# A Fourier convolution with two mixtures of experts behind it: the first batch in the planned order, weights decoded without GpSimd

## The chip, the core and the metric

The kernel runs on one core of a Trainium2 chip. TensorE (PE) multiplies, VectorE (DVE), ScalarE (ACT) and GpSimd (POOL) work on tiles, and every transfer is issued by the queue of SyncE (SP), in order. The metric is the device time of one execution in microseconds (us).

## The reference, cut to what matters

```python
X = np.fft.rfft(x, axis=1)                      # x: 8 x 3072 x 256
y = np.fft.irfft(X * (filt_r + 1j * filt_i)[None], n=3072, axis=1)
x = y.reshape(8 * 3072, 256)
h = x @ w_in                                     # 256 x 2048, float64 weights
x = (h / (1 + np.exp(-h)) @ w_out).astype(np.float32)
logits = x @ phi                                 # 32 slots, 8 experts
d = softmax(logits, axis=0); c = softmax(logits, axis=1)
slots = d.T @ x                                  # 32 x 256
slots = relu(slots[e] @ w1[e]) @ w2[e]           # for each expert e
return c @ slots
```

## The kernel before

**Fourier part.** A batch of 3072 tokens is 24 x 128. Stage 1 makes 12 products `pa` of tiles x and cosines c (128 x 256 and 128 x 128 each), folds them into `ea` and stores that in DRAM (scratch s1). Stage 2, in four quarters Q, gathers `a` from s1 (four transfers of 24 rows x 8 KB a quarter), multiplies it with `em` into four banks `px` (U = 0 to 3) and scales by the filter `f`: y = px * f_r on VectorE (direct), sw = the two halves of px exchanged and signed on ScalarE, times f_i on GpSimd (cross), and y + sw on VectorE. Stage 3 multiplies y with `gm` into four banks `pb`, copies them to `eb` and stores those in s2. Stage 4, for each chunk of 512 tokens (six a batch, 48 in all), loads `b` from s2, adds signs (`bp`, `b`, called fly in the code), multiplies with `d` into `py` and splits the result into `yT`, high and low part.

**Expert part.** For each chunk 16 blocks m of six products `ph` of yT and w_hl (w_in, split in high and low), silu `g` on ScalarE, a transpose X of g on VectorE, and the logits `pl`, 128 products of g with `wp` = w_out phi, made once. The soft mixture sums exp(logits) with X (`pd`, with the tile `E`, which comes through DRAM as `ed`) into `acc` on VectorE. After the last chunk a tail runs the experts and writes the output.

**Weights.** w_in and w_out arrive as float64, as pairs of 32-bit words. `decode` turns 512 columns (a quarter) into float32: ScalarE takes the high word's magnitude, VectorE does four operations on 128 x 1024, ScalarE converts part of the low word, and GpSimd multiplies and adds (four operations of 128 x 512). `split_w` makes w_hl. For `wp`, `make_wp` multiplies w_out (transposed) with phi, and PE transposes the same tile for the tail: it goes to DRAM as `wos` and comes back as `wo`, one transfer of 2 MB.

**Order.** A list `plan` holds (t, function); t is in slots, 16 to a chunk, and the functions run in the order of t. Each engine then works in that order, and SP issues its transfers in it. Batches 1 to 7 are planned (`fft_plan`), one batch ahead of its chunks, so that their stages stand between hidden products. Batch 0 stands as code (`fft_first`) at t = -20: for each Q it issues four gathers, then three filter loads; its products stand as px0, px1, pb0, px2, pb1, px3, pb2, pb3.

## Time and profile before

| | us |
|---|---|
| median of 3 runs | 1971.06 (1967.1 to 1977.47) |
| the profiled execution | 1971.93 |
| its span | 1970.2 |
| PE busy | 1848.9 (94% of the span) |
| DVE / ACT / POOL busy | 1287.9 / 951.0 / 340.5 |
| moved by the DMA engines | 264.36 MB, 134 GB/s on average |
| mean granted clock of PE | 0.959 of full speed |

The execution lasts 1.7 us longer than its span, which runs from the first to the last record. A share of the whole span is a mean over stages with different limits: the rows further down are therefore by stage. A row of a timeline has the start, the duration, the engine, the line, the operation with its output and input, how many instructions it joins, and in brackets how long the engine had been idle before it and what it had waited for.

### The profile page before, as it was taken

The numbers are of one execution on the slowest core, as the hardware profiler recorded it, in microseconds if no ns is written. First come the engines' busy times: TensorE is split into PE (matmuls) and PEld (weight loads), VectorE is DVE, ScalarE is ACT, GpSimd is POOL, SyncE is SP. The second block draws the span as 40 slices with busy tenths as digits, with TensorE's granted clock in tenths as the row PEclk, the third lists the DMA queues.
The fourth block names the chain that finished last, engine by engine and source line by source line (L and its number), as shares of the span: only waits on it lengthen the run. The fifth ranks groups of instructions, "written<-read, shape, count | busy, mean of one in ns | idle before, by whom it ended". The sixth has DMA issues, their size and how long they took to land. (4 is left out here: it accounts for less than half of the span.)

```text
span 1970.2 us, 49869 instructions
## 1 busy us (share of the span) xinstructions
PE 1848.9 (94%) x21108; PEld 1385.5 (70%) x21108; DVE 1287.9 (65%) x2207; ACT 951.0 (48%) x1816; POOL 340.5 (17%) x248
## 2 busy tenths in 40 slices
PE   4569999999999999999999999999999999999985
PEld 2157677877787777877777777767787777777643
DVE  4777666767767775767676776676676774555443
ACT  3444455555454564554554545545544644343322
POOL 3653211212121220221121121121121210000000
PEclk7679999999999999999999999999999999999886
DMA  9745533445254443453253533453344513311669
GB/s 280 207 176 177 127 88 106 131 135 130 57 157 130 120 116 86 144 139 105 71 176 107 131 95 110 147 150 83 102 140 125 143 54 120 100 35 37 210 234 386
DMA packets 186943, 264.36 MB, mean 134 GB/s; under 512 B 18784, under 2 KB 144096, under 8 KB 179424
## 3 DMA queue, kind: packets, MB, share of 16 engines
q1 hardware_dynamic: 186720, 261.17, 44.6%
q8 instruction: 166, 2.72, 0.6%
q14 instruction: 57, 0.47, 0.1%
HBM read 177.80 MB, written 83.30 MB: 133 GB/s over the span
## 5 line engine op out<-in xcount | busy, mean ns | idle before, releaser
L61 PE MATMUL ph<-yT,w_hl 128*128 128x512 f32 x4608 | 1096.2, 393 | 2.1 <-ACT g L593 1.7
L61 PEld LDWEIGHTS ph<-yT,w_hl 128*128 128x128 f32 x4608 | 851.4, 188 | 204.9 <-issue 25.8
L603 DVE STREAM_TRANSPOSE X<-g 128x512 f32<-128x512 f32 x768 | 515.6, 694 | 206.0 <-ACT g L593 205.6
L593 ACT ACTIVATE g<-ph 128x512 f32<-128x512 f32 x768 | 454.6, 608 | 350.0 <-PE ph L61 305.2
L237 POOL TENSOR_TENSOR sw<-sw,f 128x512 f32<-128x512 f32 x128 | 180.0, 1430 | 739.2 <-DVE X L603 346.1
L571 ACT ACTIVATE yT<-py 128x512 fp32r<-128x512 f32 x96 | 57.4, 598 | 366.9 <-PE py L61 366.9
L61 PE MATMUL pd<-X,E 32*32 32x512 f32 x6144 | 226.1, 611 | 3.5 <-DMA E<-ed 3.1
L61 PEld LDWEIGHTS pl<-g,wp 128*32 128x32 f32 x6144 | 163.4, 110 | 72.8 <-issue 50.6
L61 PE MATMUL pl<-g,wp 128*32 128x128 f32 x6144 | 191.3, 275 | 4.1 <-issue 4.0
L290 POOL TENSOR_TENSOR xh<-x,xh 128x512 fp32r<-128x512 f32 x84 | 111.9, 1333 | 465.8 <-DVE xh L289 445.7
L61 PEld LDWEIGHTS pd<-X,E 32*32 32x32 f32 x6144 | 119.4, 104 | 81.9 <-issue 46.9
L687 DVE SCALAR_TENSOR_TENSOR acc<-acc,nm,pd 128x512 f32<-128x512 f32 x188 | 127.2, 738 | 34.4 <-PE pd L61 33.9
L572 DVE TENSOR_TENSOR yT<-py,yT 128x512 fp32r<-128x512 f32 x96 | 66.4, 691 | 59.4 <-ACT yT L571 59.1
L360 DVE TENSOR_TENSOR y<-y,sw 128x512 f32<-128x512 f32 x112 | 104.8, 975 | 0.0
L61 PE MATMUL pa<-xh,ch 128*128 128x256 f32 x504 | 76.4, 287 | 9.9 <-ACT wp L146 9.7
L234 DVE TENSOR_TENSOR y<-px,f 128x512 f32<-128x512 f32 x120 | 78.9, 677 | 10.2 <-ACT sw L227 8.7
L61 PEld LDWEIGHTS pa<-xh,ch 128*128 128x128 f32 x504 | 72.4, 192 | 18.5 <-ACT wp L146 10.0
L61 PE MATMUL py<-d,b 128*128 128x128 f32 x416 | 68.4, 290 | 17.9 <-DMA b<-s 11.6
L554 DVE SCALAR_TENSOR_TENSOR bp<-b,sg 128x512 f32<-128x512 f32 (+1 forms) x48 | 34.9, 727 | 69.9 <-DMA b<-s 69.3
L226 ACT ACTIVATE sw<-px,sg 128x256 f32<-128x256 f32 x128 | 64.6, 505 | 33.0 <-DVE y L232 14.7
L633 ACT ACT_TABLE_LOAD x48 | 61.6, 1283 | 37.2 <-DVE nm L626 26.2
L61 PE MATMUL pb<-y,gm 32*32 32x512 f32 (+1 forms) x1072 | 70.1, 627 | 9.2 <-DVE y L464 5.6
(126 smaller groups left out, 1286.4 us busy)
## 6 DMA issues: line engine op xcount, KB each, us to landing
f<-in_filt_dram SPq DMA_DIRECT2D x128, 256.0 KB
x<-in_x_dram SPq DMA_DIRECT2D x96, 256.0 KB
a<-s SPq DMA_DIRECT2D x128, 192.0 KB
s<-eb SPq DMA_DIRECT2D x128, 192.0 KB
out_dram<-ots SPq DMA_DIRECT2D x40, 512.0 KB
d<-in_dmat_dram SPq DMA_DIRECT2D x48, 256.0 KB
wt<-in_w_dram SPq DMA_DIRECT2D x12, 1024.0 KB
E<-ed SPq DMA_DIRECT2D x188, 64.0 KB
```

The lines of the kernel that those rows point to most:

```text
L61: T.matmul(o, lhsT=l, rhs=r, start=start, stop=stop)
L226: A.activation(sw[:, 0, :], p[:, 1, :], AF.Copy, scale=sg[:, s:s + 1])
L234: V.tensor_tensor(y, p, f[:, 0, :].unsqueeze(1).to_broadcast([P, 2, CH]), op=ALU.mult)
L237: G.tensor_tensor(sw, sw, f[:, 1, :].unsqueeze(1).to_broadcast([P, 2, CH]), op=ALU.mult)
L290: G.tensor_tensor(h[:, 1, :], tf, h[:, 0, :], op=ALU.subtract)
L360: V.tensor_tensor(y, y, st.pop(("sw", Q, U)), op=ALU.add)
L571: A.activation(y[:, half, 0, :], py, AF.Copy)
L572: V.tensor_tensor(y[:, half, 1, :], py, y[:, half, 0, :], op=ALU.subtract)
L593: A.activation(g, pht.pop((c, m)), AF.Silu)
L603: V.transpose(xt[c][:, m].rearrange("p b j -> p (b j)"), gt[c, m])
L633: A.activation(t[:, 0], L, AF.Exp, bias=nm[:, 1:2], accum_out=nm[:, 2:3])
L687: V.scalar_tensor_tensor(out=acc[:, :, a, :], in0=acc[:, :, a, :], scalar=mrun[c][:, 3:4], in1=p, op0=ALU.mult, op1=ALU.add)
```

## The change

- **Batch 0 is planned.** `first_plan` puts every step of batch 0 in the list, by microseconds turned into slots. The gathers and filter loads alternate one by one; quarter 0 of the words of w_in is loaded before the stores of stage 1, quarter 1 between those stores and the first gather, quarters 2 and 3 behind the filters and between the stores of s2.
- **Stage 3 takes y and sw apart.** For batch 0 each is multiplied with gm, into the same banks: 32 products a quarter instead of 16, and no addition on VectorE. For U = 3 sw is made by two operations on VectorE straight from px, so GpSimd has three crosses a quarter.
- **Decoding without GpSimd.** One operation on VectorE multiplies the low word by its exponent and a second one adds; ScalarE's conversion is gone too (the magnitude on ScalarE and the four operations before it stay, now in `dec_act` and `dec_dve`). Quarter 3 of w_in and all of w_out are decoded after the first hidden products, between the transposes X, which wait for them there.
- **wp with phi standing.** Eight products of 128 columns a quarter, and one 128 x 128 transpose on VectorE. The transposes on PE, their copies on ScalarE and the way through `wos` are gone.
- **Cosines split beforehand.** Batches 1 to 7 load the high and low part (256 KB a unit instead of 128 KB); ScalarE copies both in one operation and VectorE's subtraction is gone. The tag c has two buffers instead of four, so the load of unit u stands behind the split of unit u - 2 instead of u - 3. The 12 units of batch 1 start 5.2 slots later and lie closer.
- **w_out for the tail.** Four loads of 1 MB of w_out in its own layout come in chunks 41 to 46 and are decoded there (8 operations on ScalarE, 48 on VectorE, of 128 x 512). The weights of experts 0 and 1 are loaded later.

```diff
-            ld=3, c=4, ch=2, xh=2, ev=1, a=1, f=2, sw=1, y=2, ev8=1, bl=1, bp=1, dl=1, wt=3)
+            ld=3, c=2, ch=2, xh=2, ev=1, a=1, f=2, sw=1, y=2, ev8=1, bl=1, bp=1, dl=1, wt=3)
...
-            A.activation(f, top, AF.Copy, scale=2.0 ** -36)
-            for h in range(2):
-                G.tensor_tensor(f[:, h], f[:, h], e[:, h].bitcast(F32), op=ALU.mult)
-                G.tensor_tensor(f[:, h], f[:, h], b[:, h].bitcast(F32), op=ALU.add)
...
+    def load_words(key, q):
+        for h in range(2):
+            src = w_in if key == "in" else w_outT
+            DQ.dma_start(words[key, q][:, h].rearrange("p f w -> p (f w)"),
+                         src[h * P:h * P + P, 512 * q:512 * q + 512].bitcast(U32))
...
+    def dec_low(key, q, out=None):
+        b, e = temps.pop((key, q))
+        t = words[key, q]
+        f = t[:, :, :, 0].bitcast(F32)
+        V.scalar_tensor_tensor(out=f, in0=t.bitcast(U16)[:, :, :, 1], scalar=2.0 ** -36, in1=e.bitcast(F32),
+                               op0=ALU.mult, op1=ALU.mult)
+        V.tensor_tensor(f if out is None else out, f, b.bitcast(F32), op=ALU.add)
...
-        for m in range(4):
-            for h in range(2):
-                mm(pw[:, m, :], f[:, h, m * P:(m + 1) * P], phi_f[:, h, :], h == 0, h == 1)
-        A.activation(wp[:, 4 * q:4 * q + 4, :], pw, AF.Copy)
-        for v in range(2):
-            pt = ps_f.tile([P, 2, CH], F32, tag="pf", name=f"pt_{q}{v}")
-            for m in range(2):
-                for h in range(2):
-                    o = (2 * v + m) * P
-                    T.transpose(pt[:, m, h * P:h * P + P], f[:, h, o:o + P], idt)
-            ev = wk.tile([P, 2, CH], F32, tag="E4", bufs=BUFS["E4"], name=f"wo_{q}{v}")
-            A.activation(ev, pt, AF.Copy)
-            DQ.dma_start(wos[:, 4 * q + 2 * v:4 * q + 2 * v + 2, :], ev)
...
+        f = words["out", q][:, :, :, 0].bitcast(F32).rearrange("p h (m k) -> p h m k", k=P)
+        pwt[q] = pw = ps_f.tile([P, 4 * S], F32, tag="pf", name=f"pw_{q}")
+        for h in range(2):
+            for g in range(4):
+                mm(pw[S * g:S * g + S], phi_f[:, h, :], f[:, h, :, S * g:S * g + S], h == 0, h == 1)
+    def put_wp(q):
+        V.transpose(wp[:, 4 * q:4 * q + 4, :].rearrange("p m s -> p (m s)"), pwt.pop(q))
...
+    def stage3(ps, ys, Q):
+        def special(part):
+            n = 2 * len(ys)
+            for i in range(n):
+                mm(ps[0][0:S, part, :], gm[0:S, 1 + 2 * part + i % 2, :], ys[i // 2][0][0:S, i % 2, :], i == 0, i == n - 1)
+        for i, y in enumerate(ys):
+            for U in range(4):
+                for q in range(4):
+                    if (Q, U, q) == (0, 0, 0):
+                        special(0) if i == 0 else None
+                    else:
+                        mm(ps[q][S * U:S * U + S], gm[S * q:S * q + S, 0, :], y[U][S * q:S * q + S],
+                           i == 0, i == len(ys) - 1)
         if Q == 0:
-            for n in range(1, 4):
-                special(n)
+            special(1)
...
-            c = fp.tile([P, 2, P], F32, tag="c", bufs=BUFS["c"], name=f"c_{b}_{u}")
-            DQ.dma_start(c, cmat[:, 2 * u:2 * u + 2, :])
+            c = fp.tile([P, 2, 2, P], F32, tag="c", bufs=BUFS["c"], name=f"c_{b}_{u}")
+            DQ.dma_start(c, chl[:, 2 * u:2 * u + 2])
...
-            A.activation(ch[:, 0], c, AF.Copy)
-            V.tensor_tensor(ch[:, 1], c, ch[:, 0], op=ALU.subtract)
+            A.activation(ch, c, AF.Copy)
...
-            at(max(t - 7, ts[u - 3] + 0.4) if u > 2 else t1[0] - 9 + u, load1, u)
+            at(max(t - 7, ts[u - 2] + 0.4) if u > 1 else t1[0] - 9 + u, load1, u)
...
+        def load2(Q, U):
+            gather2(st["s1"], st["aa"][:, Q], Q, U)
...
+        def act2(Q, U):
+            k = 4 * Q + U
+            tag = (("ld", "ch", "f", "ev"), ("ld", "ch", "f", "sw"))[Q % 2][U]
+            sws[k] = fp.tile([P, 2, CH], F32, tag=tag, bufs=BUFS[tag], name=f"sw_0_{k}")
+            p = ps["px", Q, U]
+            if U < 3:
+                scale_act(p, sws[k], st["f0"] if k == 0 else None)
+            else:
+                for i in range(2):
+                    V.scalar_tensor_tensor(out=sws[k][:, i, :], in0=p[:, 1 - i, :], scalar=sg[:, i:i + 1],
+                                           in1=fs[k][:, 1, :], op0=ALU.mult, op1=ALU.mult)
...
+        def mat3(Q):
+            for q in range(4):
+                ps["pb", Q, q] = ps_h.tile([P, 2, CH], F32, tag="ph", name=f"pb_0_{Q}{q}")
+            pb = [ps["pb", Q, q] for q in range(4)]
+            stage3(pb, [[t[4 * Q + U] for U in range(4)] for t in (ys, sws)], Q)
...
+                t = 22 + 0.4 * Q + 0.1 * U
+                at(us(t + 0.05), loadf, 4 * Q + U)
+                at(us(t), load2, Q, U)
...
+            t = 33 + 6.3 * Q
+            at(us(t), mat2, Q)
+            for U in range(4):
+                at(us(t + 1.2 + 0.7 * U), direct2, Q, U)
+                at(us(t + (1.3, 2.2, 3.1, 4)[U]), act2, Q, U)
+                if U < 3:
+                    at(us(t + 2.3 + 1.3 * U), cross2, Q, U)
+            t += 6.4
+            at(us(t), mat3, Q)
+            for q in range(4):
+                eng = (A, A, A, V) if Q < 3 else (A, V, A, V)
+                at(us(t + (2.3, 2.8, 3.3, 3.35)[q]), out3, Q, q, eng[q])
+            at(us(t + 4), store3, Q)
...
+        at(us(25.9), loadd, 0)
+        for q, (t0, t1, t2, t3, t4, t5) in enumerate(((5, 22, 23.2, 26.5, 29, 30.2), (21, 28.5, 31, 38.3, 44.8, 44.9),
+                                                      (43, 61, 61.9, 63, 65, 66), (49, 73, 75, 76.5, 79, 80.2))):
+            at(us(t0), load_words, "in", q)
+            at(us(t1), dec_act, "in", q, "a" if q % 2 == 0 else "xh")
+            at(us(t2), dec_dve, "in", q)
+            at(us(t3), dec_low, "in", q)
+            at(us(t4), split_act, q)
+            at(us(t5), split_dve, q)
+        at(us(62.6), load3, 0)
+        at(us(68.5), fly, 0)
+        at(us(66.1), start)
+        for q, t in enumerate((80, 84.5, 89, 92)):
+            at(us((66, 66.2, 66.3, 66.4)[q]), load_words, "out", q)
+            at(us(t), dec_act, "out", q, "a" if q % 2 == 0 else "y")
+            at(us(t + 1.2), dec_dve, "out", q)
+            at(us(t + 4.5), dec_low, "out", q)
+            at((12.5, 12.6, 17.6, 17.7)[q], make_wp, q)
+            at((12.51, 12.61, 17.61, 17.71)[q], put_wp, q)
...
-        DQ.dma_start(tail["wo"], wos)
...
+    def load_wo(q):
+        t = tail["tp"].tile([P, 2, 2048], U32, tag="wt", bufs=BUFS["wt"], name=f"words_wo{q}")
+        words["wo", q] = t[:, 0].rearrange("p (h f w) -> p h f w", h=2, w=2)
+        temps[q] = tuple(t[:, 1].rearrange("p (x h f) -> p x h f", x=2, h=2)[:, i] for i in range(2))
+        DQ.dma_start(t[:, 0].rearrange("p (m f) -> p m f", m=4),
+                     w_out[512 * q:512 * q + 512].bitcast(U32).rearrange("(m p) f -> p m f", p=P))
...
+    for q in range(4):
+        t1 = t + 1.5 + 16 * q
+        at(t1 + 2, load_wo, q)
+        for h in range(2):
+            at(t1 + 7 + h, wo_act, q, h)
+            for i in range(5):
+                at(t1 + 7.7 + h + i, wo_dve, q, h, i)
     for e in range(2):
-        at(t + 12 + 16 * e, load_w1, e, None)
-        at(t + 18 + 16 * e, load_w2, e, None)
-    at(-20, first_batch)
-    at(-18, start)
-    at(1.4, split_w, 3)
-    for q in range(4):
-        at((0.9, 3.2, 6.2, 9.2)[q], decode_wp, q)
-        at((6.4, 8.4, 12.6, 14.6)[q], make_wp, q)
+        at(t + 66 + 10 * e, load_w1, e, None)
+        at(t + 71 + 10 * e, load_w2, e, None)
```

The first place is SP's queue at the start of stage 2 of batch 0 (a is the gathered tile, f the filters). Before:

```order
L199 DMA a_0_91<-s1_0_89 24x2048 x4
L423 DMA f_0_0_221<-in_filt_dram 128x512
L423 DMA f_0_1_223<-in_filt_dram 128x512
L423 DMA f_0_2_225<-in_filt_dram 128x512
L199 DMA a_0_91<-s1_0_89 24x2048 x4
```

After:

```order
L187 DMA a_0_126<-s1_0_88 24x2048
L432 DMA f_0_0_218<-in_filt_dram 128x512
L209 DMA f0_0_220<-in_filt0_dram 128x256
L187 DMA a_0_126<-s1_0_88 24x2048
L432 DMA f_0_1_223<-in_filt_dram 128x512
L187 DMA a_0_126<-s1_0_88 24x2048
L432 DMA f_0_2_226<-in_filt_dram 128x512
L187 DMA a_0_126<-s1_0_88 24x2048
L432 DMA f_0_3_229<-in_filt_dram 128x512
```

Four gathers no longer stand ahead of a group of three filters; each gather is followed by the filter of the same number.

The second place is ScalarE in stages 2 and 3 of batch 0, around the copies of the first pb. Before:

```order
L226 ACTIVATE sw_0_6_372<-px_0_12_338,sg_79 128x256
L227 ACTIVATE sw_0_6_372<-px_0_12_338,sg_79 128x256
L226 ACTIVATE sw_0_7_379<-px_0_13_339,sg_79 128x256
L227 ACTIVATE sw_0_7_379<-px_0_13_339,sg_79 128x256
L477 ACTIVATE eb_0_0_411<-pb_0_00_388 128x512
L477 ACTIVATE eb_0_0_411<-pb_0_01_389 128x512
L477 ACTIVATE eb_0_0_411<-pb_0_02_390 128x512
L477 ACTIVATE eb_0_0_411<-pb_0_03_391 128x512
L226 ACTIVATE sw_0_8_440<-px_0_20_420,sg_79 128x256
```

After:

```order
L214 ACTIVATE sw_0_5_400<-px_0_11_332,sg_79 128x256
L215 ACTIVATE sw_0_5_400<-px_0_11_332,sg_79 128x256
L482 ACTIVATE eb_0_0_404<-pb_0_00_351 128x512
L482 ACTIVATE eb_0_0_404<-pb_0_01_352 128x512
L214 ACTIVATE sw_0_6_409<-px_0_12_333,sg_79 128x256
L215 ACTIVATE sw_0_6_409<-px_0_12_333,sg_79 128x256
L482 ACTIVATE eb_0_0_404<-pb_0_02_353 128x512
L126 ACTIVATE w_hl_75<-words_in_125 128x2x512
L214 ACTIVATE sw_0_8_487<-px_0_20_429,sg_79 128x256
```

The sw of U = 2 of the next quarter has moved behind two copies of pb, so it stands behind all products into those banks; the sw of U = 3 is gone from ScalarE.

The third place is VectorE from the end of w_in's decoding on, in chunk 0 (db_out, de_out: w_out's decoding, X: transposes, xh_1_0: first tile of batch 1). Before:

```order
L128 TENSOR_TENSOR w_hl_75<-words_in_168,w_hl_75 128x2x512
L603 STREAM_TRANSPOSE X_0_705<-g_0_0_694 128x512
L603 STREAM_TRANSPOSE X_0_705<-g_0_1_707 128x512
L114 TENSOR_SCALAR db_out1_726<-db_out1_726 128x1024
L115 TENSOR_SCALAR db_out1_726<-db_out1_726 128x1024
L116 SCALAR_TENSOR_TENSOR db_out1_726<-words_out_639,db_out1_726 128x1024
L117 TENSOR_SCALAR db_out1_726<-db_out1_726 128x1024
L603 STREAM_TRANSPOSE X_0_705<-g_0_2_717 128x512
L286 TENSOR_TENSOR ch_1_0_738<-c_1_0_651,ch_1_0_738 128x256
L289 CAST xh_1_0_741<-x_1_0_649 128x512
```

After:

```order
L130 TENSOR_TENSOR w_hl_75<-acc_80,w_hl_75 128x2x512
L617 STREAM_TRANSPOSE X_0_759<-g_0_0_707 128x512
L112 TENSOR_SCALAR db_out0_756<-db_out0_756 128x1024
L113 TENSOR_SCALAR db_out0_756<-db_out0_756 128x1024
L114 SCALAR_TENSOR_TENSOR db_out0_756<-a_0_126,db_out0_756 128x1024
L115 TENSOR_SCALAR db_out0_756<-db_out0_756 128x1024
L617 STREAM_TRANSPOSE X_0_759<-g_0_1_720 128x512
L617 STREAM_TRANSPOSE X_0_759<-g_0_2_733 128x512
L617 STREAM_TRANSPOSE X_0_759<-g_0_3_747 128x512
L121 SCALAR_TENSOR_TENSOR a_0_126<-a_0_126,db_out0_756 128x1024
L123 TENSOR_TENSOR a_0_126<-a_0_126,db_out0_756 128x1024
L617 STREAM_TRANSPOSE X_0_759<-g_0_4_761 128x512
```

The two operations of L121 and L123 that replace GpSimd's four now stand between the transposes; xh_1_0, nine rows behind w_in's last subtraction (L128) before, stands eighteen rows behind it (L130) now, since the next quarter's decoding lies ahead of it too.

## Rows read from the trace of the kernel before

**Rows 1.** Windows of the whole core, by stage:

```profile
core 0: us, PE busy (x) PEld busy (x) DVE busy (x) ACT busy (x) POOL busy (x), PEclk, DMA share, GB/s
24.00:31.50 7.50, 0.00 (x0) 0.00 (x0) 2.89 (x4) 4.15 (x4) 0.00 (x0) 0.50 0.99 363
31.50:60.00 28.50, 18.21 (x105) 3.61 (x106) 18.75 (x19) 8.08 (x18) 22.13 (x15) 0.50 0.91 202
104.00:202.00 98.00, 76.96 (x669) 65.03 (x668) 70.17 (x105) 44.87 (x81) 39.08 (x28) 0.88 0.50 160
202.00:1640.00 1438.00, 1427.54 (x16828) 1086.79 (x16828) 988.81 (x1737) 746.75 (x1448) 251.72 (x184) 1.00 0.42 118
1640.00:1860.00 220.00, 213.74 (x2504) 167.55 (x2502) 119.29 (x207) 90.86 (x159) 0.00 (x0) 0.98 0.26 84
```

**Rows 2.** Timeline of the DMA queue on SP, stages 2 and 3 of batch 0:

```profile
34.36 3.53 SPq L199 DMA_DIRECT2D a<-s  x4
...
42.15 3.58 SPq L199 DMA_DIRECT2D a<-s  x4
...
72.36 18.58 SPq L264 DMA_DIRECT2D s<-eb  x12
94.22 0.39 SPq L539 DMA_DIRECT2D b<-s  x1
```

**Rows 3.** Timeline of PE, start of the program:

```profile
36.03 6.08 PE L61 MATMUL px<-a,em 24*32 24x512 f32 x36 [0.28 <-DMA a<-s]
...
81.13 4.54 PE L61 MATMUL pb<-y,gm 32*32 32x512 f32 x32 [1.17 <-ACT eb L477]
97.32 0.76 PE L61 MATMUL py<-d,b 128*128 128x128 f32 x2 [11.65 <-DMA b<-s]
...
103.88 1.56 PE L61 MATMUL ph<-yT,w_hl 128*128 128x512 f32 x4
...
128.52 1.65 PE L61 MATMUL pa<-xh,ch 128*128 128x256 f32 x6 [9.69 <-ACT wp L146]
```

**Rows 4.** Timeline of PE, batch 1 and the marker:

```profile
201.69 1.22 PE L61 MATMUL py<-d,bp 128*128 128x128 f32 x4
...
206.01 1.91 PE L61 MATMUL px<-a,em 24*32 24x256 f32 x38
```

**Rows 5.** Groups by line and shape: products and transposes for the logit weights:

```profile
L61 PE MATMUL pw<-phi_f,words_out 128*128 128x32 f32 x64 | 8.0, 277 | 1.1 <-POOL words_out L121 1.1
...
L152 PE MATMUL pt<-idt,words_out 128*128 128x128 f32 x32 | 5.7, 321 | 2.6 <-DVE ea L190 2.6
```

**Rows 6.** Timeline of PE around the stall in chunk 40:

```profile
1645.28 5.76 PE L61 MATMUL pd<-X,E 32*32 32x512 f32 x83 [3.11 <-DMA E<-ed]
```

**Rows 7.** Timeline of VectorE, decoding with and without GpSimd beside it:

```profile
28.50 0.69 DVE L114 TENSOR_SCALAR db_in<-db_in 128x1024 f32<-128x1024 f32 x1 [7.83 <-ACT db_in L113]
...
29.96 1.23 DVE L116 SCALAR_TENSOR_TENSOR db_in<-words_in,db_in 128x1024 uint32<-128x1024 uint32 x1
...
32.55 1.66 DVE L115 TENSOR_SCALAR db_in<-db_in 128x1024 uint32<-128x1024 uint32 x1
```

**Rows 8.** Timeline of VectorE, last eviction of batch 0 and a transpose:

```profile
86.94 1.28 DVE L475 COPY eb<-pb 128x512 f32<-128x512 f32 x2
...
120.30 0.70 DVE L603 STREAM_TRANSPOSE X<-g 128x512 f32<-128x512 f32 x1
```

**Rows 9.** Timelines of ScalarE and GpSimd, batch 0:

```profile
63.57 0.47 ACT L226 ACTIVATE sw<-px,sg 128x256 f32<-128x256 f32 x1 [0.37 <-PE px L61]
...
80.48 2.06 ACT L477 ACTIVATE eb<-pb 128x512 f32<-128x512 f32 x4
...
67.31 4.63 POOL L237 TENSOR_TENSOR sw<-sw,f 128x512 f32<-128x512 f32 x3 [1.56 <-ACT sw L227]
```

**Rows 10.** Load of a cosine tile on SP and its split on ScalarE, batch 5:

```profile
1006.34 0.41 SPq L279 DMA_DIRECT2D c<-in_cmat_dram  x1
...
1012.18 0.41 ACT L285 ACTIVATE ch<-c 128x256 fp32r<-128x256 f32 x1
```

More of the change, by code (lines that the diff above doesn't have):

```diff
@@ new lines, in store3 @@
+        def store3(Q):
+            store2(st["s2"], es.pop(Q), Q)
+        at(us(-5), begin)
+        for v in range(6):
+            at(us(-4 + 0.1 * v), load, v)
+        at(us(-3), alloc)
+        at(us(-2.9), load_small)
+        for u in range(12):
+            t = 6 + u + (1 if u else 0)
+            at(us(t), mat1, u)
+            at(us(t + 1.2), out1, u)
+            at(us(t + 2), sums1, u)
+        for u, n, t in ((0, 4, 13.4), (4, 4, 17), (8, 2, 18.9), (10, 2, 20.6)):
+            at(us(t), store1, u, n)
```

305 lines of the change are left out of this document (131 added, 174 removed).

## Prediction

> **What bounds the kernel now.** I read the windows by stage first. From 202 to 1640 us PE is busy 1427.5 of 1438 us at the full clock, while VectorE is busy 988.8 and the DMA engines 42% [rows 1]: there only PE's own work counts, and the change takes none away. What can move lies at the two ends. From 31.5 to 60 us the DMA engines are 91% busy but move 202 GB/s, where they had moved 363 just before, and PE works 18.2 of 28.5 us at half clock [rows 1]. From 104 to 202 us PE is busy 77 of 98 us [rows 1].
>
> The timelines say which wait ends last in each stretch. SP's queue: a second group of four gathers is issued at 34.36, the third at 42.15, so four gathers and three filters take 7.8 us [rows 2]. PE's queue: the first quarter's products end at 42.1 and took 6.08 us, though 38 such records take 1.91 at the full clock [rows 3, 4], so 3.6 at half; the other 2.5 us waited for the last gathers, and the first set was complete near 39. The last stores of stage 3 are issued from 72.36 to 90.9, the load of b at 94.22 [rows 2]; PE waits 11.65 us for it and makes the first hidden product at 103.88 [rows 3]. In chunk 0 PE waits 9.69 us for the copy of wp [rows 3], and late, at 1645, 3.11 us for E [rows 6]. My marker for the start is the first product of chunk 2's stage 4, at 201.69 [rows 4]; between it and the first hidden product lie 97.8 us.
>
> **The change, part by part. 1. To the first hidden product.** Ahead of the first gather both orders put 2 MB of words, so I leave the first set at 39. A quarter now has a fourth filter with its gathers. One filter is 0.26 MB, 0.7 us at 363 GB/s [rows 1]; the set takes 7.8 + 0.7 = 8.5 us, and the sets are complete at 39, 47.5, 56 and 64.5.
>
> Against that stands the cycle of the engines. A quarter of px is 1.9 us at the full clock [rows 4]. The last 16 products pb took 4.54 us at half clock [rows 3], so 2.3 at full, and 32 of them 4.5. Two copies of pb on ScalarE take 1.1 (four took 2.06), and a sw of two halves 0.8 to 0.9 [rows 9]. In ScalarE's new order the sw of U = 2 stands behind two copies of pb, so the next px cannot begin before pb is done: the cycle is 1.9 + 4.5 + 1.1 + 0.8 = 8.3 us, about the pace of the loads. GpSimd's three crosses, 4.63 us [rows 9], lie beside it; the added products cost 2.3 us a quarter, and the addition on VectorE that they replace lay in the same chain. Which clock? PE was granted 0.50 from 31.5 to 60 us, where it was idle a third of the time, 0.88 from 104 to 202 and 1.00 where it was busy throughout [rows 1]. Between 1.9 and 3.8 us for px, and 4.5 and 9.1 for pb, I take half for the first quarter and full from the second on, where PE works 6.4 of 8.3 us, nearer to the 77 of 98 at 0.88; half throughout is a rival.
>
> Then px1 ends at 50, pb0 at 56 (part of it at half clock), px2 at 59.5, pb1 at 64, px3 at 67.3 (behind its set and 1.9 + 1.9), pb2 at 71.8, pb3 at 76.4, and the last copies at 78.6 (two for each of two engines). Before, the last copy ended at 88.2 [rows 8], 15.7 us ahead of the first hidden product. The same road (store, load of b, signs, py) stays; VectorE's signs lose GpSimd as a neighbour, for which I take 1 us. The first hidden product comes at 78.6 + 15.7 - 1 = 93.3: a gain of 10.6 us. The words q2 and q3 now stand in SP's queue ahead of stores; 2 MB at 363 GB/s are 5.6 us, which lie in the 20 us from 64.5 to 85 with 3.1 MB of stores (8.7 us).
>
> **2. From there to the marker.** The products pw and transposes pt, 8.0 + 5.7 us of PE [rows 5], become about 2 us. But VectorE sets the pace now. Before xh_1_0 it has, behind the first yT: nine operations of the kind of 0.69 us, eight of the kind of 1.23 [rows 7], seven transposes of 0.70 [rows 8] and a cast of 0.4: 6.2 + 9.8 + 4.9 + 0.4 = 21.3 us. It starts 1.7 us behind the first hidden product; with 1.5 us for waits on ScalarE it is at +24.5. PE has twelve blocks of products to do until then (about 17.7 us) and waits. The two operations on w_out's second quarter, then the third quarter's first four, and the short transposes bring wp at +35.4, and the first logits with it. The third and fourth quarters, between folds, casts and transposes, bring the rest of wp at +57.8. From about +60 PE has 22.7 us of its own work left to the marker, so +82 to +86; I take 84. Before it was 97.8: a gain of 13.8 us. Nothing of it is hidden, since PE is what waits at both places.
>
> **3. Elsewhere.** The load of wo (2 MB) stood ahead of E in the queue; the first late load of w_out now stands behind it, so the 3.1 us [rows 6] go. Its decoding is 48 operations, half of each kind above at half the width: 24 x 0.35 + 24 x 0.62 = 23 us; it lies in chunks where VectorE is busy 119 of 220 us [rows 1], so I take nothing; without that cover it costs up to 23 us. The cosine tiles bring 0.13 MB more for each of 84 units, under DMA engines that are 42% busy. Their load is issued later, behind the split of the unit two before; now it leaves SP at 1006.34 and is split at 1012.18, 5.8 us later [rows 10], and with the new place some 5.4 us remain. I take nothing. VectorE's subtraction and ScalarE's changed copy cost nothing or save nothing, under PE.
>
> **Sum.** 10.6 + 13.8 + 3.1 = 27.5 us off the profiled execution of 1971.93 gives 1944.4. That execution lay 0.9 us above the median of the runs, so about **1944 us**.
>
> **The rivals.** *B, gathers faster than their pace now.* If the alternation lets every transfer go at 363 GB/s, a set (1.83 MB) takes 5.1 us and only the cycle counts: the first set is there near 36, pb0 ends at 47.5, and three cycles of 8.3 us and the copies bring the last one at 70 to 71, the first hidden product at 85.5. That is 7.8 us less: 1936. For it: the gathers held the engines busy at 202 GB/s while few bytes moved. Against: a gather has the same 24 rows as before. The Trainium skill, "DMA: Bandwidth & Descriptors", section "Why a DMA increments its semaphore by 16 and not by 1", says that a transfer is divided over the largest number of engines up to 16 that divides its outer size, 12 for 24 rows; by that rule 0.2 MB takes 12/16 of the full rate, an estimate of 0.7 us, and the gathers' slower pace is not their own. The row of 202 GB/s with the engines 91% busy does not bear that out.
>
> *C, half clock through stages 2 and 3.* The cycle is 3.8 + 9.1 + 1.9 = 14.8 us. From pb0's end at 59 the last copy comes near 100, the first hidden product at 114.6, 10.7 us later than before; with the other gains 1965. For it: the clock is 0.50 from 31.5 to 60 [rows 1]. Against: the larger share of work now.
>
> *D, VectorE lengthened by GpSimd.* An operation of 0.69 us took 1.66 beside GpSimd [rows 7]. Batch 1's twelve units give GpSimd twelve operations of the crosses' size inside part 2, 18.5 us at 1.54 [rows 9]; at that ratio VectorE loses 10.8 us of them, and all 18.5 if it stands still: 1955 to 1962. For it: VectorE is the bound there. Against: the crosses and decoding on GpSimd that lengthened it before are gone. The Trainium skill, "SBUF — State Buffer", section "Who interferes with whom", calls the port that the two share an exclusive lock under which the loser stands still; by that rule the time would be 1962. The row (0.69 to 1.66) shows a long wait but not a full one.
>
> *E, the other side: cosine tiles late.* If the load of 256 KB behind a nearer split comes late, ScalarE's queue stops and with it silu, and PE. To end slower than before by more than 0.5% it must eat the 27.5 us and 9.9 more, 0.45 us for each of 84 units: above 1981. The 5.4 us that remain speak against it; it decides when a load takes longer than that.
>
> *F, the late decoding is not covered*: up to 23 us, 1967, no change that can be told.
>
> **How the numbers follow.** My own case 0.54, B 0.20, C 0.11, D 0.08, E 0.04, F 0.03. Within 0.5% (1961 to 1981), about what a measurement can tell from no change, lie F, most of C and little else: 0.11. Slower holds E and a little for several of the others at once: 0.06. Faster is the rest, 0.83. My case alone reaches from 1932 (a cycle begun earlier, +82) to 1956 (one quarter more at half clock, 6.5 us, and some of D). The range reaches to B at 1936 with the same play below it, and to the edge of C: 1920 to 1966.
>
> **What would show it.** In the profile after: gathers and filters 8 to 9 us apart by quarter; the first hidden product at 93; px and pb at the full clock from the second quarter; the first pl about 35 us behind it, at 129, released by VectorE; the marker at 177; no wait for E at 1620; PE idle for some 10 us in all from there to 1600 (1438 - 1427.5 before). A first hidden product at 85 or 114 says B or C; a marker more than 90 us behind it, with xh's low parts on GpSimd beside long VectorE rows, says D; idle time of PE behind ScalarE's copies of c says E.

## The result, and the profile after

The changed kernel takes 1946.0 us (median of 4 runs, 1941.1 to 1948.7) against 1970.3 us: ratio 0.9869, 95% interval 0.9835 to 0.9903. The profiled execution took 1945.7 us, its span is 1943.9. The forecast was 1944. The total came out, but a third of the gain did not come from where it was put.

The windows of the changed kernel, in the columns of [rows 1] (the third stretch ends at the first sums of chunk 0, the fourth at those of chunk 38):

```profile
30.00:60.00 30.00, 17.92 (x143) 5.20 (x144) 14.44 (x18) 6.00 (x12) 6.69 (x5) 0.51 0.95 196
60.00:84.00 24.00, 19.11 (x248) 6.39 (x256) 10.62 (x18) 11.05 (x24) 9.32 (x8) 0.72 0.90 254
102.00:179.50 77.50, 61.88 (x445) 48.80 (x444) 65.54 (x105) 38.54 (x65) 15.37 (x12) 0.92 0.52 175
179.50:1552.40 1372.90, 1365.85 (x16199) 1039.34 (x16199) 928.43 (x1599) 727.88 (x1385) 244.98 (x180) 1.00 0.46 128
```

The first row answers to the one of 31.5 to 60 us in [rows 1]: the DMA engines are 95% busy instead of 91%, and move 196 GB/s instead of 202. In the fourth PE is idle 7.1 us of 1372.9. The same stretch of the kernel before, from the first sums of chunk 0 to those of chunk 38:

```profile
191.88:1573.89 1382.01, 1368.96 (x16198) 1041.64 (x16197) 950.25 (x1671) 712.95 (x1385) 246.13 (x180) 1.00 0.43 120
```

There PE was idle 13.1 us, and the same number of its records took 1369.0 us instead of 1365.9.

PE's timeline, from the first gathered tile to the marker (stage 4 of chunk 2, 201.69 before [rows 4]):

```profile
34.83 1.03 PE L62 MATMUL px<-a,em 24*32 24x256 f32 x2 [15.10 <-DMA a<-s]
...
43.65 2.86 PE L62 MATMUL px<-a,em 24*32 24x512 f32 x32 [0.92 <-DMA a<-s]
...
54.24 1.15 PE L62 MATMUL px<-a,em 24*32 24x512 f32 x13 [0.79 <-DMA a<-s]
...
74.70 1.14 PE L62 MATMUL px<-a,em 24*32 24x512 f32 x13 [1.32 <-DMA a<-s]
...
96.20 0.79 PE L62 MATMUL py<-d,b 128*128 128x128 f32 x2 [11.17 <-DMA b<-s]
...
102.25 17.47 PE L62 MATMUL ph<-yT,w_hl 128*128 128x512 f32 x72
...
126.31 0.55 PE L62 MATMUL pa<-xh,ch 128*128 128x256 f32 x1 [6.59 <-DVE xh L270]
...
136.62 2.48 PE L62 MATMUL pl<-g,wp 128*32 128x128 f32 x64 [3.28 <-DVE wp L146]
...
185.82 0.71 PE L62 MATMUL py<-d,bp 128*128 128x128 f32 x4
```

PE waits for the last gather of the first quarter until 43.65 and for the last one of the fourth until 74.70; in [rows 3] the first quarter's products had ended at 42.1. The first hidden product starts at 102.25, against 103.88 [rows 3]. From there on it is quicker: the wait of 9.69 us for wp [rows 3] is now 6.59 us for xh and 3.28 for wp, both released by VectorE, the first logits come 34.4 us behind the first hidden product and the marker 83.6 us.

SP's queue in the same stretch, the first gather of the second, third and fourth quarter, and the first load of b:

```profile
35.62 0.32 SPq L187 DMA_DIRECT2D a<-s  x1
...
46.18 0.32 SPq L187 DMA_DIRECT2D a<-s  x1
...
56.86 0.32 SPq L187 DMA_DIRECT2D a<-s  x1
...
93.13 0.39 SPq L553 DMA_DIRECT2D b<-s  x1
```

The quarters are 10.6 and 10.7 us apart, where the groups of [rows 2] were 7.8. The starts of groups on PE's timeline split the whole gain (in us; "sums" of a chunk means the start of its first product pd):

| stretch | before | after | gain |
|---|---|---|---|
| to the first hidden product | 103.9 | 102.3 | 1.6 |
| to the sums of chunk 0 | 88.0 | 77.2 | 10.8 |
| chunk 0 to chunk 38 | 1382.0 | 1372.9 | 9.1 |
| chunk 38 to chunk 40 | 71.4 | 68.1 | 3.3 |
| chunk 40 to chunk 46 | 196.2 | 197.2 | -1.0 |
| from there to the end | 128.7 | 126.2 | 2.5 |

### The profile page after: what moved, and what is told of

Same layout as the page of the kernel before. It is cut to its first block, busy times and chain, and to the rows that moved or that the text cites. A ratio compares the mean times of both kernels' runs of the same rounds, so it can differ in the third digit from the quotient of the medians.

```text
span 1943.9 us, 49938 instructions
## 1 busy us (share of the span) xinstructions
PE 1832.9 (94%) x21210; PEld 1373.7 (71%) x21210; DVE 1271.4 (65%) x2186; ACT 954.2 (49%) x1793; POOL 282.2 (15%) x212
## 5 line engine op out<-in xcount | busy, mean ns | idle before, releaser
L225 POOL TENSOR_TENSOR sw<-sw,f 128x512 f32<-128x512 f32 x124 | 171.7, 1408 | 793.1 <-ACT sw L215 299.5
L62 PE MATMUL pd<-X,E 32*32 32x512 f32 x6144 | 220.3, 601 | 0.9 <-issue 0.9
L701 DVE SCALAR_TENSOR_TENSOR acc<-acc,nm,pd 128x512 f32<-128x512 f32 x188 | 127.1, 737 | 44.3 <-PE pd L62 44.3
L62 PE MATMUL px<-a,em 24*32 24x512 f32 (+1 forms) x1072 | 66.3, 643 | 26.7 <-DMA a<-s 21.0
L647 ACT ACT_TABLE_LOAD x48 | 61.6, 1283 | 38.6 <-DVE nm L640 27.1
L62 PE MATMUL py<-d,b 128*128 128x128 f32 x416 | 65.9, 282 | 13.3 <-DMA b<-s 11.2
```

The costliest lines, as they stand in the source:

```text
L62: T.matmul(o, lhsT=l, rhs=r, start=start, stop=stop)
L225: G.tensor_tensor(sw, sw, f[:, 1, :].unsqueeze(1).to_broadcast([P, 2, CH]), op=ALU.mult)
L647: A.activation(t[:, 0], L, AF.Exp, bias=nm[:, 1:2], accum_out=nm[:, 2:3])
L701: V.scalar_tensor_tensor(out=acc[:, :, a, :], in0=acc[:, :, a, :], scalar=mrun[c][:, 3:4], in1=p, op0=ALU.mult, op1=ALU.add)
```

## The experiments

One profiled execution of each, by the same stretches (us), and the median where several runs were timed ("to hidden" is the time to the first hidden product, "rest" that from the sums of chunk 46 to the end). Brackets behind a median hold its ratio to the kernel before and the 95% interval:

| kernel | to hidden | to chunk 0 | 0 to 38 | 38 to 40 | 40 to 46 | rest | median |
|---|---|---|---|---|---|---|---|
| e1_grouped | 95.6 | 78.1 | 1376.0 | 68.3 | 197.8 | 131.2 | 1946.7 |
| e2_gathers_alone | 89.9 | 77.3 | 1380.1 | 68.7 | 197.4 | 128.5 | |
| e3_filters_alone | 90.4 | 77.3 | 1374.9 | 68.4 | 197.3 | 128.4 | |
| e4_cosine_on_vector | 96.9 | 82.9 | 1374.2 | 68.6 | 197.3 | 128.5 | 1951.1 |
| b1_wo_behind_E | 104.0 | 88.6 | 1384.7 | 68.2 | 199.9 | 132.2 | 1971.6 |
| e5_grouped_wo_ahead | 96.4 | 77.2 | 1374.5 | 68.4 | 196.4 | 128.5 | |
| e6_sum_before_stage3 | 98.3 | 77.3 | 1371.4 | 68.1 | 198.3 | 128.0 | 1943.9 |
| e7_low_on_gpsimd | 98.2 | 88.0 | 1374.0 | 68.4 | 197.1 | 127.9 | 1955.2 |
| e8_lead_of_three | 95.4 | 83.9 | 1375.8 | 68.4 | 199.4 | 128.8 | 1953.9 |
| e9_words_later | 98.9 | 77.3 | 1373.7 | 68.2 | 197.2 | 129.2 | 1946.4 |
| e10_high_words_only | 104.7 | 77.1 | 1373.6 | 68.3 | 195.4 | 127.1 | |
| e11_words_later_2 | 94.6 | 78.2 | 1376.2 | 68.5 | 197.5 | 130.1 | 1944.0 |

**e1_grouped.** The filters of a quarter behind its four gathers.

```diff
-                at(us(t + 0.05), loadf, 4 * Q + U)
+                at(us(22.35 + 0.4 * Q + 0.01 * U), loadf, 4 * Q + U)
```

> The changed kernel, with the loads of stage 2 of batch 0 in groups again: the four gathers of a quarter, then its four filters, instead of one gather and one filter in turn. Nothing else differs. In the changed kernel the last gathers of the four quarters are there near 43.6, 54, 65 and 74.7 us, 10.4 us a quarter, and the first hidden product starts at 102.3. Theory 'order': gathers in turn with filters pass more slowly than four gathers side by side. Then the quarters are 8.5 us apart (7.8 for four gathers and three filters before, and 0.7 for one more filter), the first set is complete near 39, the last near 65, the first hidden product starts at 93 to 95 and the kernel ends 7 to 9 us earlier than the changed one, near 1937. Rival 'amount': the bytes and rows take their time in any order (more of them are in flight while PE, VectorE and the words wait for the same engines). Then the quarters stay 10 us apart, the first hidden product within 2 us of 102.3 and the time within 3 us of 1946.

The first hidden product came at 95.6, as "order" had it, but the median, 1946.7 (0.9863, 0.9845 to 0.9882), as "amount" had it. Later kernels with the same loads as the changed one decide: gathers and filters in turn gave a first hidden product at 102.3 and then, in e4, e6, e7, e8 and e10, at 96.9, 98.3, 98.2, 95.4 and 104.7 (e6 has another stage 3 as well); the grouped order 95.6 and 96.4. The spread of one order is 9 us, so what was taken for the order is mostly the execution. The order does show in the first quarter. Grouped, its products are over at 42.1 us, as in the kernel before [rows 3], and at 42.3 in e5:

```profile
35.19 6.94 PE L62 MATMUL px<-a,em 24*32 24x256 f32 x38 [15.32 <-DMA a<-s]
```

In turn they are over at 46.5 in the changed kernel and between 44.9 and 47.6 in the seven other kernels that begin with that order (e2 and e3 too): the quarter's fourth gather stands behind three filters there. By the first hidden product nothing is left of this; at 219 GB/s it comes at 95.4 and 96.9 in turn and at 95.6 grouped. What differs between executions shows in the DMA columns from 29 to 63 us, of e10 and e4 (same order) and e1 (grouped):

```profile
29.00:63.00 34.00, 19.43 (x150) 5.54 (x150) 15.92 (x21) 6.83 (x14) 7.20 (x5) 0.54 0.93 191
```

```profile
29.00:63.00 34.00, 22.33 (x201) 7.42 (x216) 17.55 (x23) 9.31 (x18) 8.48 (x6) 0.55 0.92 219
```

```profile
29.00:63.00 34.00, 22.97 (x242) 7.53 (x242) 20.18 (x27) 12.27 (x26) 10.53 (x8) 0.65 0.95 219
```

The engines are busy for nearly the same share (0.93, 0.92, 0.95) and move 191, 219 and 219 GB/s; e10's first hidden product is the latest of all, the other two are among the early ones.

**e2_gathers_alone and e3_filters_alone.** One kernel leaves out the filter loads of quarters 1 to 3, the other their gathers.

```diff
+            if k > 3:
+                fs[k] = fs[k % 4]
+                return
...
+            if Q == 0:
+                gather2(st["s1"], st["aa"][:, Q], Q, U)
```

> The changed kernel, which leaves out the filter loads of quarters 1 to 3 of batch 0 (those quarters are scaled with the filter of the first one), so that twelve gathers follow each other in the queue alone. This prices a gather by itself. Theory 'order' and the price that the prediction used: 7.8 us less three filters of 0.7 us leaves 5.7 us for four gathers side by side, so quarters 1 to 3 arrive 5.7 us apart and PE is held by its own cycle of 8.3 us. Rival 'amount': four gathers take 7.5 us or more whatever stands beside them (10.4 less four filters of 0.7 us), and the quarters arrive 7.5 us apart.

> The changed kernel, which leaves out the gathers of quarters 1 to 3 of batch 0 (all quarters multiply the first one's tile), so that twelve filter loads follow each other alone. This prices a filter by itself, 0.26 MB. Theory 'order': 0.7 us each (363 GB/s), so the sixteen filters are issued within about 12 us of the first set, and PE runs at its own cycle, 8.3 us a quarter at the full clock, first hidden product near 85. Rival 'amount': the same price for a filter, since only gathers are slow. If a filter takes more than 0.9 us by itself, the part of the sum that gave 0.7 us for it was wrong. At 14.8 us a quarter the half clock, and not the loads, would hold PE.

SP's queue, twelve gathers in a row in e2, and thirteen filters in a row in e3:

```profile
36.90 12.97 SPq L187 DMA_DIRECT2D a<-s  x12
```

```profile
35.80 18.64 SPq L432 DMA_DIRECT2D f<-in_filt_dram  x13
```

A gather took 12.97 / 12 = 1.08 us, 4.3 for four: cheaper than the 5.7 that the sum implied. The 18.64 us of the filters are no such price, since SP also waited for buffers in them (us in total, times, longest), and until 44.7 us the first quarter's gathers were still on their way:

```profile
SPq L432 <- POOL sw L225: 3.6, 2, 2.6
...
SPq L432 <- DVE y L219: 2.5, 1, 2.5
```

A stretch of each kernel in which only the one kind was on its way gives the pace, gathers in e2 and filters in e3:

```profile
46.00:50.00 4.00, 2.22 (x6) 0.46 (x6) 3.30 (x8) 2.30 (x6) 1.53 (x2) 0.50 0.81 184
```

```profile
45.00:48.00 3.00, 2.56 (x32) 0.69 (x4) 0.41 (x2) 0.00 (x0) 0.00 (x0) 0.50 1.00 361
```

At 361 GB/s a filter takes 0.73 us, so the prediction's 0.7 was right for a filter by itself. By themselves four gathers and four filters make 4.3 + 2.9 = 7.2 us a quarter. Together they never came so fast: in the six executions of the order in turn the first gathers of quarters stand 8.4 to 11.2 us apart. Neither kind alone has the slow pace; it comes with the mixture, and its size differs from one execution to the next. Why was not shown.

In both kernels the first hidden product came at 90: with half of the loads gone it came some 9 us earlier than the mean of 99.3 in the six executions with all of them, and still behind rival B's 85.5. PE's own cycle shows there: px of the fourth quarter begins 6.8 and 6.9 us behind that of the third (56.54 to 63.29, 56.68 to 63.59). The Trainium skill, "DMA: Bandwidth & Descriptors", section "Why a DMA increments its semaphore by 16 and not by 1", has a rule by which 24 rows go to 12 engines. The engines' busy share with gathers alone, 0.81, is not far from 12 of 16, but the estimate of 0.7 us a gather by that rule is not borne out by 1.08.

**e4_cosine_on_vector and e8_lead_of_three.** The old split of the cosines (128 KB a unit); in e8 also four buffers and the old lead of the loads (the last pair of lines).

```diff
...
-            A.activation(ch, c, AF.Copy)
+            A.activation(ch[:, :, 0], c, AF.Copy)
+            V.tensor_tensor(ch[:, :, 1], c, ch[:, :, 0], op=ALU.subtract)
...
-            at(max(t - 7, ts[u - 2] + 0.4) if u > 1 else t1[0] - 9 + u, load1, u)
+            at(max(t - 7, ts[u - 3] + 0.4) if u > 2 else t1[0] - 9 + u, load1, u)
```

> The changed kernel, with the old split of the cosines: 128 KB a unit is loaded, ScalarE copies the high part and VectorE subtracts to get the low part; the two buffers and the order stay. Between the sums of chunk 1 and chunk 39 the changed kernel was 8.7 us faster than the one before, which the prediction did not have. Theory 'VectorE': the 84 subtractions stood in VectorE's queue, each behind a copy on ScalarE, and made PE wait for acc (4.6 us in three places, then half clock behind one of them). Undone, that wait is back: 5 to 9 us slower than the changed kernel, near 1952. Rival 'chance': the places where PE waits for acc fall differently in each program or run; then this kernel is within 2 us of the changed one between the same chunks.

> The changed kernel with the whole part on the cosines undone: the old split with VectorE's subtraction (as in e4_cosine_on_vector) and also four buffers of c and the load of unit u behind the split of unit u - 3. From the sums of chunk 0 to those of chunk 38 the kernel before took 1382.0 and 1384.7 us in two looks, the changed kernel 1372.9, and e4, with the subtraction alone undone, 1374.2. In the kernel before, one more load of x and c stands in SP's queue ahead of E and b, and b's first use comes 5.9 us behind the sums of chunk 16 instead of 4.7. Theory 'queue': that earlier load is what made b late and PE wait; with the old lead the stretch takes 1380 to 1385 us again, and the median is 6 to 10 us above e4's, near 1958. Rival 'chance' or another part of the change: the stretch stays at 1371 to 1377, and the median near e4's 1951.

Both medians rose against the changed kernel's, by 5 and 8 us, but not where "VectorE" and "queue" had put it: chunk 0 to chunk 38 stayed at 1374.2 and 1375.8, as the rival had it both times. The subtraction costs in chunk 0, where the stretch to its sums went from 77.2 to 82.9 and 83.9. PE's waits there, in the changed kernel and in e4 (in total, times, longest):

```profile
PE pa L62 <- DVE xh L270: 6.6, 1, 6.6
```

```profile
PE pa L62 <- DVE xh L271: 9.1, 4, 6.9
```

Twelve subtractions of about 0.4 us lie in VectorE's queue there, and PE waits for the casts behind them: VectorE sets the pace of that stretch. So the 9 us between chunks 0 and 38 are not the cosines' doing; "VectorE" and "queue" both fall for them.

**b1_wo_behind_E.** The kernel before, with one transfer moved.

```diff
+    def load_wo():
         DQ.dma_start(tail["wo"], wos)
...
+    at(t + 3.5, load_wo)
```

> The kernel before, with one transfer moved: the 2 MB of wo for the tail are issued behind E and the next b in chunk 40 instead of ahead of E. Everything else is as before. Theory 'queue': PE's wait of 3.1 us for E came from those 2 MB, so the time from the sums of chunk 38 to those of chunk 40 falls from 71.4 us to 68.3 and the kernel is 3 us faster, near 1969. Rival: E is late for another reason, and the 71.4 us stay. It is also a second look at the kernel before between chunk 0 and chunk 38 (1382.0 us there, 1372.9 in the changed kernel). Theory 'chance' for that difference of 9 us: it is another number here, by some us either way. Theory 'VectorE': it is 1380 to 1384 again, since the subtractions are still there.

E's wait went (68.2), and the time did not: 1971.6 (1.0005, 0.999 to 1.0021). PE stood at the next place instead, at a product that reads d, whose load the 2 MB now stand ahead of (the trace names no releaser for this wait):

```profile
1656.24 0.77 PE L61 MATMUL py<-d,b 128*128 128x128 f32 x2 [3.86 <-issue]
```

Chunk 40 to 46 rose by 3.7 us. The wait had only moved. So "queue" was right about E and wrong about the time. As a second execution with the old start (1979.4 us, the longest of its ten) it gave 104.0 us to the first hidden product and 1384.7 from chunk 0 to 38.

**e5_grouped_wo_ahead.** The grouped order, and 1 MB of w_out ahead of E.

```diff
-        at(t1 + 2, load_wo, q)
+        at(t + 2.1 if q == 0 else t1 + 2, load_wo, q)
```

> The changed kernel, with two edits in stretches far apart: the loads of stage 2 of batch 0 in groups of four gathers and four filters, and the first late load of w_out (1 MB) ahead of E in chunk 40 again. Start: a second look at the grouped order, whose first hidden product came at 95.6, against 102.3 and 96.9 in two looks at the order in turn. Theory 'the pace differs from run to run': anything from 94 to 102. Theory 'order': 95 to 96 again. Chunk 40: theory 'queue': 1 MB is 2.8 us at 363 GB/s, half of the transfer that cost 3.1 us, so the time from the sums of chunk 38 to those of chunk 40 rises from 68.3 to between 69 and 70. Rival: it stays at 68.3 because 1 MB is over before E is wanted.

The rival holds: 68.4 us, and PE does not wait for E. 1 MB ahead of E costs nothing, where 2 MB had made PE wait 3.11 us [rows 6]. So the new place was not needed; with 2 MB, b1 shows that the place alone would have freed E as well.

**e6_sum_before_stage3.** Sums on VectorE and 16 products a quarter.

```diff
+                V.tensor_tensor(ys[k], ys[k], sws[k], op=ALU.add)
+            stage3(pb, [[ys[4 * Q + U] for U in range(4)]], Q)
```

> The changed kernel, with stage 3 of batch 0 as it was: VectorE adds y and sw (four operations a quarter), PE multiplies the sum, 16 products a quarter instead of 32. By the prediction's cycle, doubled products cost PE 2.3 us a quarter at the full clock and the additions cost VectorE 4 x 0.7 to 4 x 1.2 us, of which some lies behind the crosses. Theory 'loads': the quarters are held by the gathers and filters, the cycle does not matter, and the first hidden product comes within the spread of the changed kernel (97 to 102), the median within 2 us of 1946. Theory 'cycle': PE's 2.3 us a quarter were on the path, and the first hidden product comes 4 to 6 us earlier, near 93. Theory 'chain': VectorE's additions stand between the last cross and pb, and it comes 4 us later.

98.3 us and 1943.9 (0.9858, 0.983 to 0.9885): nearest to "loads", with a median that cannot be told from 1946.0. But this execution had the fastest loads of the six (222 GB/s from 29 to 63 us), and at 219 the first hidden product came at 96.9 and 95.4 in e4 and e8. At the end PE waits for an addition:

```profile
77.52 3.95 PE L62 MATMUL pb<-y,gm 32*32 32x512 f32 x32 [3.20 <-DVE y L476]
```

So VectorE's additions do come onto the path in the last quarter once the loads are quick, and the halved products save 2.3 us a quarter by the prediction; how far the two cancel was not shown. The changed kernel waits 0.67 us there, for ScalarE's copy.

**e7_low_on_gpsimd.** The low words of five quarters on ScalarE and GpSimd again.

```diff
+        if key == "out" or q == 3:
+            A.activation(f, t.bitcast(U16)[:, :, :, 1], AF.Copy, scale=2.0 ** -36)
+            for h in range(2):
+                G.tensor_tensor(f[:, h], f[:, h], e[:, h].bitcast(F32), op=ALU.mult)
+                G.tensor_tensor(f[:, h], f[:, h], b[:, h].bitcast(F32), op=ALU.add)
+            return
```

> The changed kernel, with the low words of w_in's last quarter and of all of w_out converted on ScalarE and multiplied and added on GpSimd again (four operations of 128 x 512 a quarter), in place of the two operations on VectorE; the order of everything else stays. Theory 'VectorE sets the pace in chunk 0' and GpSimd is idle there: VectorE loses 5 x 2.46 = 12.3 us of work, and if GpSimd's four operations (5.2 to 6.4 us a quarter) run beside it without harm, the time from the first hidden product to the sums of chunk 0, 77 us, falls by up to 8. Theory 'lock': VectorE's operations beside GpSimd last longer (0.69 took 1.66), and each quarter's wp waits for a longer chain: the first logits come 4 us or more later than 34.4 us behind the first hidden product, and the time to the sums of chunk 0 rises to 82 or more, the kernel to 1950 or more.

"Lock" holds: 88.0 us to the sums of chunk 0, the number of the kernel before, the first logits 38.6 us behind the first hidden product, and 1955.2 (0.9907, 0.9871 to 0.9942). VectorE beside GpSimd in that stretch, and what PE waits for:

```profile
129.55 1.68 DVE L113 TENSOR_SCALAR db_out<-db_out 128x1024 uint32<-128x1024 uint32 x1
131.27 2.19 DVE L114 SCALAR_TENSOR_TENSOR db_out<-a,db_out 128x1024 uint32<-128x1024 uint32 x1
```

```profile
124.85 0.55 PE L62 MATMUL pa<-xh,ch 128*128 128x256 f32 x1 [5.24 <-DVE xh L276]
...
134.66 0.66 PE L62 MATMUL pw<-a,phi_f 128*32 128x128 f32 x8 [3.49 <-POOL a L125]
```

The operations of 0.69 and 1.23 us [rows 7] take 1.68 and 2.19. GpSimd's rows at that time:

```profile
129.04 1.64 POOL L125 TENSOR_TENSOR a<-a,db_out 128x512 f32<-128x512 f32 x1
130.64 1.74 POOL L124 TENSOR_TENSOR a<-a,de_out 128x512 f32<-128x512 f32 x1
```

Each of the two operations of VectorE starts while one of GpSimd is under way and ends 0.55 and 1.08 us behind that one's end (130.68 and 132.38), less than it takes by itself: as if it had stood until GpSimd was through. The Trainium skill, "SBUF — State Buffer", section "Who interferes with whom", calls the shared port an exclusive lock. These rows agree with it.

The 5.24 us for xh end ahead of these rows and are less than the 6.59 of the changed kernel; xh comes 26.7 us behind the first hidden product instead of 24.1, and two operations ahead of it had taken 1.77 and 1.66 us instead of 0.69. PE waits 3.49 us for GpSimd's own last addition, and for the low parts of xh, which stand in GpSimd's queue behind the low words, 6.3 us where the changed kernel has 3.2 (total, times, longest):

```profile
PE pa L62 <- POOL xh L277: 6.3, 4, 3.4
```

So the longer VectorE rows are one part of the loss, and the longer chain through GpSimd another.

**e9_words_later.** Grouped, and 1 MB of w_in's words moved behind the last filter (of the changed line, the one tuple).

```diff
-                    (21, 28.5, 31, 38.3, 44.8, 44.9)
+                    (25.8, 49.7, 50, 57, 61.65, 61.7)
```

> The changed kernel, with the loads of stage 2 in groups, and quarter 1 of w_in's words loaded behind the last filter instead of ahead of the first gather; it is decoded in VectorE's gaps in the third and fourth quarter and behind the last copies. Theory 'loads set the pace up to the first hidden product': 1 MB at 363 GB/s is 2.9 us, the gathers start that much earlier, the first set is complete near 37, and the first hidden product comes at 92 to 94 instead of 95.6 and 96.4 in the two looks at the grouped order; the median is 1941 to 1943. Rival 'VectorE': the decoding (6.8 us) now stands between y of the last quarter, the last copies and the signs of b, and the first hidden product stays at 96 or comes later.

The first hidden product came at 98.9, the median is 1946.4. PE began the first quarter 2.6 us earlier than in e1 (32.58 against 35.19), as "loads" had it, and lost it again for a reason that neither theory had. ScalarE's first decoding operation stood in its queue before the words had come, and the copies of pb behind it:

```profile
68.90 1.12 ACT L107 ACTIVATE db_in<-words_in 128x1024 f32<-128x1024 f32 x1 [8.63 <-DMA words_in<-in_w_in_dram]
```

```profile
76.21 2.85 PE L62 MATMUL pb<-y,gm 32*32 32x512 f32 x19 [7.28 <-ACT eb L482]
```

**e11_words_later_2.** As e9, and the decoding moved behind that work.

```diff
-                    (25.8, 49.7, 50, 57, 61.65, 61.7)
+                    (25.8, 55.95, 56, 61.7, 61.75, 61.8)
```

> As e9_words_later (grouped loads, quarter 1 of w_in's words behind the last filter), but that quarter is decoded behind VectorE's and ScalarE's work on the third quarter's banks, when its words have landed. In e9 they landed at 68.9 us and ScalarE stood at their decoding for 8.6 us, with the copies and sw behind it: pb of the last quarter waited 7.3 us for them, and the first hidden product came at 98.9, although the first set of gathers was there 3 us earlier. Theory 'loads': without that stall pb of the last quarter ends near 74, the last copies near 76, and the first hidden product comes at 90 to 93, 3 to 6 us ahead of the grouped order alone (95.6, 96.4); median 1938 to 1942. Rival 'VectorE': two quarters' decoding, 13.6 us, between the last copies and the signs of b takes it back: the first hidden product stays at 95 or later and the median at 1944 or more.

94.6 us and 1944.0 (0.9865, 0.9843 to 0.9888), below the changed kernel by less than the two can be told apart. The last copies ended at 78.0, 2.5 us earlier than in e1 (80.5), the first hidden product came 1.0 earlier. PE waits for b and then for the signs, which stand in VectorE's queue behind 13 us of decoding:

```profile
88.41 0.79 PE L62 MATMUL py<-d,b 128*128 128x128 f32 x2 [14.02 <-DMA b<-s]
91.48 0.79 PE L62 MATMUL py<-d,bp 128*128 128x128 f32 x2 [2.28 <-DVE bp L568]
```

Against e1, whose wait for the signs is 0.69 us, 1.6 us go there. That fits the rival, but does not show it: in the changed kernel the same wait is 2.15 us, with VectorE idle ahead of the signs until b had come.

**e10_high_words_only.** No decoding of w_out for the tail; the high words are copied.

```diff
-            V.tensor_tensor(o, f, b.bitcast(F32), op=ALU.add)
+            V.tensor_copy(o, t[:, :, 1].bitcast(F32))
...
-            at(t1 + 7 + h, wo_act, q, h)
-            for i in range(5):
-                at(t1 + 7.7 + h + i, wo_dve, q, h, i)
+            at(t1 + 11.7 + h, wo_dve, q, h, 4)
```

> The changed kernel, which leaves out the decoding of w_out for the tail: one copy of the high words on VectorE stands for it (8 operations instead of 48, none on ScalarE). It prices the late decoding. From the sums of chunk 40 to those of chunk 46 the changed kernel takes 197.2 us and the one before 196.2, with one wait of 1.7 us for a silu behind it. Theory 'covered': the decoding lies under PE, and the stretch takes 196 to 197.5. Rival 'not covered': it falls to 195 or less. The start is as in the changed kernel, a further look at the pace of the loads: first hidden product between 96 and 103.

195.4 us instead of 197.2, between the two theories. The stretch took 196.4 to 199.4 us in the eleven other executions with the late decoding, so this one lies 1 us below the lowest; about 1.8 us are not covered. The changed kernel's timeline shows nearly all of it as one wait of PE for silu, whose ScalarE also has the decoding:

```profile
1746.22 3.96 PE L62 MATMUL ph<-yT,w_hl 128*128 128x512 f32 x16 [1.66 <-ACT g L607]
```

In e10 PE has no such wait between 1640 and 1830 us.

## Why the prediction came out, step by step

**To the first hidden product, 10.6 us forecast, 1.6 in the profiled execution.** The step that failed is the start and the pace of the loads: sets at 39, 47.5, 56 and 64.5 were forecast, and the first was there at 43.7, the last at 74.7. That the loads and not PE would hold this stretch was right, as e2 with e3 shows. Three things were wrong in the term. The first set was left at 39, which the grouped order keeps and the new one does not (e1). The pace was 7.8 + 0.7, with a filter priced as if it were alone; beside gathers a quarter took 8.4 to 11.2 us. And one execution's pace was taken for the next one's: six of this order give 95.4 to 104.7, at 191 to 222 GB/s. Their mean is 99.3, a gain of 4.6: of the 9.0 us that are missing, 3.0 are this execution's, and 6.0 are missing on average too. In the kernel before the spread could not be seen: its two executions give 103.9 and 104.0. The road behind the loads (15.7 us less 1) was right: 102.25 less the last copies' end at 87.2 is 15.0.

The clock was forecast as full from the second quarter on; granted were 0.51 from 30 to 60 us and 0.72 from 60 to 84. In e2 and e3 the cycle took 6.8 and 6.9 us instead of the 8.3 of the sum all the same, so the sum priced the cycle too high; in the changed kernel the loads set this stretch.

**From there to the marker, 13.8 us forecast, 14.2 measured.** Right, and shown: xh at +24.1 (+24.5 forecast), the first logits at +34.4 (+35.4), the marker at +83.6 (+84), the waits released by VectorE. e4 puts 12 subtractions into VectorE's queue, and the stretch follows.

**E, 3.1 us forecast, 3.3 measured.** Right in size, and b1 bears out that the 2 MB ahead of E were the cause. That the next load now stands behind E was not needed, though: 1 MB ahead of it costs nothing (e5), and 2 MB behind it cost as much at the next place (b1).

**Elsewhere, nothing forecast.** The late decoding costs about 1.8 us (e10). Chunk 0 to 38 gained 9.1 us that no step had, and that made good the 9.0 which the loads withheld: that the total lies within 2 us of the forecast is luck. Two executions with the old start took 1382 and 1385 there, eleven at kernels with the new start 1371 to 1376, and one 1380. Of the 9.1 us, 6.0 are less idle time of PE (13.1 to 7.1) and 3.1 are the same number of records in less time. Part of the idle time is PE's wait for acc, here before and after (total, times, longest):

```profile
PE py L61 <- DVE acc L687: 4.6, 3, 2.6
```

```profile
PE py L62 <- DVE acc L701: 0.4, 1, 0.4
```

It is 4.9 us in b1 and anything from 0.4 to 3.6 in the kernels with the new start, and e3, which has the 3.6, takes 1374.9 us all the same; so it is not the whole cause. Which part of the change it is stays open: e8 undoes the part on the cosines and keeps the gain. That batch 1 starts later, and that the batches then start at other moments relative to one another, was not tried.

**The rivals.** B's earlier first hidden product (85.5) was not reached even with half of the loads left out (90). C did not happen: the granted clock was 0.72 from 60 to 84 us, and the cycle was not the bound. D did not happen in the changed kernel, and part of e7's loss is of its kind. Its row of 0.69 us that took 1.66 was read as not a full wait; GpSimd's operation across it ran from 32.06 to 33.67 and VectorE's ended 0.54 us later, so it fits a full one too. E: with the cosines undone e8 is 8 us slower and not faster. F: about 1.8 of its 23 us are paid.

## What to carry to other kernels

A term read from one execution's transfers deserves a range of its own: here the same queue gave 191 to 222 GB/s from one execution to the next, and the time to the first hidden product spread by 9 us with it. A price taken from one kind of transfer alone need not hold beside another kind: by themselves the loads of a quarter come to 7.2 us, together to 8.4 and more. When a wait for a transfer is removed by moving another one, ask who stands behind it next: here 2 MB made the same wait at the next place, and 1 MB made none. Where one engine sets the pace of a short stretch, a neighbour that "helps" can cost more than its help: moving five quarters' low words off VectorE made the stretch 10.8 us longer.
